# Softmax sums inverted by a power on GpSimd in fifteen slots, with a new table of the first 25 slots

## The chip, the core and the metric

The kernel runs on one core of a Trainium2 chip. The core has a tensor engine for matmuls (TensorE, PE in the profile, with its weight loads as PEld), VectorE (DVE), ScalarE (ACT), GpSimd (POOL), and queues for DMA transfers; here the SyncE queue (SP) issues nearly all of those. Each engine takes its own instructions strictly in the order in which they were issued to it, and waits where an input of the next one isn't there yet. The metric is the time of one execution on the device in microseconds, as the median of several runs. Lower is better.

## What is computed

The reference is an attention that keeps the 32 largest scores of each row, followed by a feed-forward block. Cut to what matters:

```python
# q, k, v: 8 batches, 8 heads, 576 rows, 64 wide
scores = np.matmul(q, k.transpose(0, 1, 3, 2)) / np.sqrt(64)
kth = np.partition(scores, -32, axis=-1)[..., -32:-31]
scores = np.where(scores >= kth, scores, -1e9)
attn = np.exp(scores - np.max(scores, axis=-1, keepdims=True))
attn = attn / (np.sum(attn, axis=-1, keepdims=True) + 1e-09)
x = np.matmul(attn, v)              # rearranged to 4608 rows of 512
h = x @ w_in                        # 512 x 2048
out = (h / (1 + np.exp(-1.702 * h))) @ w_out
```

The division by the sum (plus 1e-09) is the step that the change touches.

## The kernel before

**Slots.** The attention is cut into 144 slots of 128 query rows for two heads each, 18 per batch. For slot n, TensorE makes two heads' scores against all 576 keys (`scores`, line 468), in two PSUM banks of 288 keys each. ScalarE copies the second bank to SBUF, and the first too (`copy_scores`, 482; the tile `sc`, four buffers). VectorE pairs the two halves by maximum and minimum (`pair_up`, 489; tile `ranked`): this needs the scores of the first bank and ScalarE's copy of the second, and when it and the copies are done, the banks are free for the scores of a later slot. Then VectorE finds the 32 largest of each row in four rounds of MAX8 and MATCH_REPLACE8 (`topk`, 509; tile `top`). This search is most of VectorE's work.

**From the search to the values.** GpSimd works out the cut and the offset for the exponential (`bounds`, 534; tiles `cut` and `low`). ScalarE masks (`mask`, 549) and takes the exponentials (`exps`, 557; tile `pr`) and gives their sums (`den`). Then comes `invert` (568): GpSimd adds 1e-09 to the sums (tile `some`, 128x2), and VectorE takes the reciprocal (tile `rden`, 128x2). In slots 0 to 8 (`BY_DMA` is 8) `rden` goes into two diagonal matrices, and TensorE normalizes while it transposes the probabilities (`divide`, 575, and `turn`, 590). From slot 9 on GpSimd normalizes (`normalize`, 582, two passes over `pr`), ScalarE splits the result into 16-bit halves into the buffer of `sc` (`split`, 618), a DMA writes these to memory (`rows<-sc`), and a transposed read brings them back (`turn_by_dma`, 626, `pt<-rows`). The buffer of `sc` is free for the copy of a slot four later when that write has read it. TensorE multiplies with the values (`values`, 652, and its variants).

**The feed-forward block** runs beside it: blocks of 128 rows of x are multiplied with `w_in` in units (`hidden`, 789), ScalarE takes a tanh (`tanh`, 814), GpSimd or VectorE gate it (`gate`, 826) and form the sums of one step of Strassen's scheme (`combine`, 843), and TensorE multiplies with `w_out` or with sums of its quarters (`project`, 896). In the first slots the weights are loaded in pieces and rounded by ScalarE, GpSimd and VectorE (`round_piece`, 265), GpSimd then forms the sums of the quarters (`weight_sums`, 875), and TensorE fills its idle time with matmuls that nothing uses (`stay_warm`, 299).

**What sets the order.** The opening and slots 0 to 24 (`COLLECTED` is 25, line 33) are recorded: every call of an engine is put into a list of 2593 steps (lines 127 to 136), and `issue_in_order` (1678) then issues them in the order that the string `ORDER` (36) writes out, a table of step numbers and runs. An engine so gets its instructions in the order of the table. From slot 25 on the calls are issued as the program makes them, in pairs of slots (`joined_pair`, 1599). In the profile a recorded step has the line L133, every later one L132, so the two parts can be told apart.

In the recorded part, `invert(n)` is called in the middle of the search of slot n + 1 (`find`, 1303, or `slot`, 1174), and its two operations are two steps that the table places apart from each other.

Of the kernel before, what the change touches and what calls it, by code (L numbers as in the profile page):

```python
# [9 lines left out]
ALU = mybir.AluOpType  # L10
ENG = mybir.EngineType
F32 = mybir.dt.float32
# [7 lines left out]
P = 128  # L20
# [12 lines left out]
COLLECTED = 25  # L33
# [112 lines left out]
def kernel(  # L146
# [27 lines left out]
    nc = Engines(tc.nc)  # L174
# [25 lines left out]
    BY_DMA = 8  # L200
# [50 lines left out]


    pieces = [(c, g) for g in range(NG) for c in range(CC)] + [(None, f) for f in range(FC)]
    raw = {}

    def load_piece(n):
        c, g = pieces[n]
# [1480 lines left out]
```

## Time and profile before

| | |
|---|---|
| median of 3 runs | 1342.28 us (1342.17 to 1343.64) |
| profiled execution | 1342.64 us, its span 1340.9 us |
| mean granted clock of TensorE | 0.996 |
| PE, DVE, ACT, POOL busy | 1326.5, 1266.9, 1158.4, 978.6 us |
| last VectorE instruction of the table ends | 241.7 us |
| reciprocals on VectorE | 144: 24 at L133, 120 at L132 |

Busy time counts an engine from the start to the end of each instruction. Matmuls are pipelined and overlap, so a TensorE that is busy all the time can still have room; the number of passes in a stretch tells more. The span runs from the first to the last instruction; the execution has 1.7 us around it. A timeline row gives start, length, engine, line, operation, output and inputs, shapes and count, and in brackets the idle time of the engine just before it and what ended it. A row of waits gives who waited for whom, and then the total, the number of times and the longest.

### The profile page before, as it was taken

The page shows a single profiled execution, that of the slowest core. Times are in us where ns is not written, and L with a number is a line of the kernel's source. Part 1 is how long each engine was busy: PE and PEld are TensorE (multiplying, and loading weights), DVE is VectorE, ACT ScalarE, POOL GpSimd, SP SyncE. Part 2 cuts the span into 40 slices and gives each one's busy share as a digit, 9 for nine tenths or more (in the row PEclk, how much of TensorE's full clock was granted, in tenths as well). Part 3 has the DMA queues.
Part 4 walks back from the last instruction along what each step waited for, and adds up shares of the span by engine and source line. Part 5 has one row for each costly group of instructions (what it writes and reads, how often), then busy time and mean ns, then how long its engine had stood idle before and what let it go on. Part 6 is the DMA issues. An engine that isn't in the chain of part 4 may idle for free.

```text
span 1340.9 us, 54139 instructions
## 1 busy us (share of the span) xinstructions
PE 1326.5 (99%) x22528; PEld 1202.9 (90%) x22528; DVE 1266.9 (94%) x3371; ACT 1158.4 (86%) x1871; POOL 978.6 (73%) x1788
## 2 busy tenths in 40 slices
PE   8999999999999999999999999999999999999998
PEld 5777689899999999999999999999999999999998
DVE  7999999999999999999999999999999999999902
ACT  6999998999999988999999989899998988888831
POOL 3888987777777777777777777777777777777761
PEclk8999999999999999999999999999999999999999
DMA  7553878888998798989999787988999878755650
GB/s 239 173 169 119 191 182 201 213 191 205 218 219 195 169 206 195 236 191 202 205 220 205 184 188 181 235 199 195 186 228 214 199 158 170 189 140 145 149 116 18
DMA packets 532358, 249.27 MB, mean 186 GB/s; under 512 B 463760, under 2 KB 510352, under 8 KB 532112
## 3 DMA queue, kind: packets, MB, share of 16 engines
q1 hardware_dynamic: 531520, 245.38, 78.5%
q8 instruction: 176, 2.88, 0.9%
q14 instruction: 70, 0.57, 0.1%
q10 hardware_dynamic: 592, 0.43, 0.1%
HBM read 46.01 MB, written 104.60 MB: 112 GB/s over the span
## 4 chain that ended last, share of the span: by engine, by line
PE 94%; DVE 3%; DMA 1%; ACT 1%; SPq 1%; issue 0%; POOL 0%; DVEq 0%; ACTq 0%; POOLq 0%
PE unit L132 32%; PE po L132 29%; PE mixed L132 12%; PE s_ps L132 7%; PE po L133 6%; PE s_ps L133 2%; PE o L133 2%; PE tp L133 2%; PE ph L133 2%; DVE ranked L133 1%; DVE top L133 1%; DMA pt<-rows 1%; ACT sc L133 1%; DMA rows<-sc 0%; SPq L133 0%
## 5 line engine op out<-in xcount | busy, mean ns | idle before, releaser
L132 DVE MAX8 top<-ranked 128x8 f32<-128x288 f32 (+1 forms) x952 | 518.2, 596 | 0.0
L132 PE MATMUL unit<-xT,win 128*64 128x128 f32 x7936 | 454.3, 273 | 0.0
L132 PEld LDWEIGHTS unit<-xT,win 128*64 128x64 f32 x7936 | 437.4, 137 | 0.0
L132 DVE MATCH_REPLACE8 ranked<-top,ranked 128x288 f32<-128x288 f32 x714 | 384.1, 543 | 0.0
L132 PE MATMUL po<-wout,th 128*64 128x128 f32 x4032 | 330.0, 274 | 0.0
L132 POOL TENSOR_TENSOR th<-th,th 128x128 f32<-128x128 f32 x374 | 273.9, 732 | 29.9
L132 PE MATMUL po<-raws,th 128*64 128x128 f32 x3064 | 252.9, 273 | 0.0
L132 PEld LDWEIGHTS po<-wout,th 128*64 128x64 f32 x4032 | 238.3, 137 | 9.9 <-issue 5.1
L132 POOL TENSOR_SCALAR pr<-pr,rden 128x576 f32<-128x576 f32 x240 | 176.5, 745 | 75.2 <-DVE rden L132 75.2
L132 ACT COPY sc<-pr 128x2304 uint16<-128x2304 uint16 x96 | 205.5, 2140 | 1.2 <-POOL pr L132 1.2
L132 PEld LDWEIGHTS po<-raws,th 128*64 128x64 f32 x3064 | 184.6, 137 | 0.0
L132 ACT ACTIVATE th<-unit 128x512 f32<-128x512 f32 x124 | 74.9, 604 | 94.4 <-PE unit L132 94.4
L132 ACT ACTIVATE pr<-sc,low 128x576 f32<-128x576 f32 x192 | 148.1, 786 | 0.0
L132 ACT ACTIVATE sc<-sc,cut 128x576 f32<-128x576 f32 x192 | 140.7, 797 | 0.0
L132 PE MATMUL s_ps<-qk_t 64*64 64x512 f32 x936 | 139.1, 596 | 1.4 <-ACT sc L133 0.8
L132 POOL TENSOR_SCALAR some<-den 128x2 f32<-128x2 f32 x120 | 26.5, 220 | 155.7 <-ACT pr L132 155.4
L132 DVE TENSOR_TENSOR ranked<-s_ps,sc 128x576 f32<-128x576 f32 x188 | 132.8, 748 | 0.0
L132 ACT COPY sc<-s_ps 128x1024 f32<-128x1024 f32 x93 | 95.6, 1028 | 33.8 <-PE s_ps L132 33.7
L132 POOL TENSOR_TENSOR th<-th 128x128 f32<-128x128 f32 x250 | 114.8, 459 | 0.4
L133 DVE MAX8 top<-ranked 128x8 f32<-128x576 f32 (+1 forms) x200 | 111.6, 598 | 0.0
L132 POOL TENSOR_TENSOR raws<-raws 128x128 f32<-128x128 f32 (+1 forms) x160 | 89.7, 569 | 8.1 <-ACT raws L132 3.0
L132 POOL TENSOR_SCALAR th<-th 128x512 f32<-128x512 f32 x124 | 76.5, 617 | 13.1 <-ACT th L132 13.1
(145 smaller groups left out, 2196.6 us busy)
## 6 DMA issues: line engine op xcount, KB each, us to landing
rows<-sc SPq DMA_DIRECT2D x112, 576.0 KB, 3.7
rows<-spare SPq DMA_DIRECT2D x24, 576.0 KB, 3.6
qk_rows<-pr SPq DMA_DIRECT2D x23, 576.0 KB, 4.9
out_dram<-raws SPq DMA_DIRECT2D x66, 128.0 KB, 3.1
raws<-in_moe_w_in_dram SPq DMA_DIRECT2D x16, 512.0 KB, 4.9
raws<-in_moe_w_out_dram SPq DMA_DIRECT2D x16, 512.0 KB, 3.8
qk_l<-in_q_dram SPq DMA_DIRECT2D x28, 256.0 KB, 4.6
qk_l<-in_k_dram SPq DMA_DIRECT2D x28, 256.0 KB, 4.8
```

The costliest lines, as they stand in the source:

```text
L132: return do(*args, **kwargs)
L133: self.engines.collected.append(lambda: do(*args, **kwargs))
```

## The change

There are two edits. In `invert`, for slots 9 to 23, the reciprocal on VectorE becomes a power on GpSimd, with an exponent tile of minus ones that is filled once at the start. Slots 0 to 8, and 24 and later, keep the reciprocal. And the table is another one: its first 165 steps are the same, and from there the 2593 steps, which are the same steps by number, stand in another order, by up to 201 places, on average 18 places away.

```diff
     pieces = [(c, g) for g in range(NG) for c in range(CC)] + [(None, f) for f in range(FC)]
     raw = {}
+    minus_one = const.tile([P, 2], F32, name="minus_one")
+    nc.gpsimd.memset(minus_one[:], -1.0)
...
         some = small.tile([P, 2], F32, name="some", tag="sums")
         nc.gpsimd.tensor_scalar(some[:], st[n]["den"][:], 1e-9, None, op0=ALU.add)
         rden = st[n]["rden"] = small.tile([P, 2], F32, name="rden", tag="inverse")
-        nc.vector.reciprocal(rden[:], some[:])
+        if BY_DMA < n < COLLECTED - 1:
+            nc.gpsimd.tensor_tensor(out=rden[:], in0=some[:], in1=minus_one[:], op=ALU.pow)
+        else:
+            nc.vector.reciprocal(rden[:], some[:])
```

The first lines of the table that differ, cut:

```diff
-208+4 130 163 156 213+4 166 157 131 167 159 132 194 191 168
+208+4 130 163 156 213+4 167 157 172+3 131 166 158 132 175 191 168
...
```

The order of the DMAs on the SP queue is the same row by row. On the other engines the order differs throughout the recorded part. What the prediction says of the new order it takes from the two orders written out engine by engine; for example, three of the places that it speaks of:

| ahead of it, number of steps | before | after |
|---|---|---|
| matmuls ahead of the last score of slot 8's first bank | 321 | 306 |
| the same for slot 10 | 402 | 386 |
| the same for slot 11 | 443 | 439 |
| ScalarE steps ahead of the copy of slot 24's second bank | 326 | 331 |
| VectorE steps, the 15 left out, ahead of slot 24's pairing | 422 | 428 |

160 rows, old and new, of the table ORDER are left out of this document.

## The prediction

> **What bounds the kernel now.** First the page: the head, the busy times and the chain of work that ended last.
>
> ```profile
> span 1340.9 us, 54139 instructions
> PE 1326.5 (99%) x22528; PEld 1202.9 (90%) x22528; DVE 1266.9 (94%) x3371; ACT 1158.4 (86%) x1871; POOL 978.6 (73%) x1788
> PE 94%; DVE 3%; DMA 1%; ACT 1%; SPq 1%; issue 0%; POOL 0%; DVEq 0%; ACTq 0%; POOLq 0%
> ```
>
> The chain is nearly all TensorE. But the change lies in the part that the table orders, and that part must be read by itself. A helper's line tells the two apart: what the table issues stands at L133, everything later at L132. Three stretches, two in the table and one across its end:
>
> ```profile
> 20.00:110.00 90.00, 85.15 (x717) 62.20 (x715) 87.70 (x236) 84.97 (x167) 77.61 (x100) 0.96 0.55 175
> 110.00:180.00 70.00, 70.00 (x685) 50.27 (x679) 69.61 (x187) 68.47 (x120) 63.69 (x85) 1.00 0.71 182
> 180.00:246.00 66.00, 64.43 (x1172) 57.14 (x1168) 64.89 (x174) 60.15 (x95) 50.44 (x93) 1.00 0.78 189
> ```
>
> The columns are PE, PEld, DVE, ACT, POOL. In 110 to 180 us VectorE works 69.61 of 70 us and ScalarE 68.47. TensorE's full figure hides room: 685 matmul passes in 70 us against 1172 in the next 66. So in the table VectorE sets the pace, with ScalarE close behind. Then the chain of waits across the end of the table, in order of time (start, length, what):
>
> ```profile
> 219.73 2.01 ACT sc L133
> 221.76 4.57 DMA rows<-sc
> 226.43 0.65 ACT sc L133
> 227.10 1.19 DVE ranked L133 x2
> ...
> 244.37 1.85 DVE ranked L132 x4
> ...
> 246.27 1.09 PE s_ps L132 x8
> ```
>
> From 227.10 to 246.2 us the chain is VectorE, row after row; TensorE starts its scores at 246.27, right after VectorE has paired slot 26. From there on the chain is TensorE's, which has most of the 94% above. What VectorE gains up to 246 can therefore become gain of the whole kernel, one for one, as long as TensorE and ScalarE can also be there earlier. What VectorE waits for in the table:
>
> ```profile
> DVE ranked L133 <- PE s_ps L133: 1.5, 3, 1.0
> DVE ranked L133 <- ACT sc L133: 1.5, 2, 0.9
> DVE wout L133 <- ACT wout L133: 0.4, 1, 0.4
> DVE rden L133 <- POOL some L133: 0.2, 1, 0.2
> DVE win L133 <- POOL win L133: 0.2, 1, 0.2
> ```
>
> That is 3.8 us after the first 20 us, and all that a better order could take from VectorE.
>
> **The change, part by part.** Removed: 15 of the reciprocals that stand in VectorE's queue.
>
> ```profile
> L133 DVE RECIPROCAL rden<-some x16: 144/152/167, 111.5 to 236.8; 128x2 f32<-128x2 f32 x16
> ```
>
> ```profile
> 129.44 0.15 DVE L133 RECIPROCAL rden<-some 128x2 f32<-128x2 f32 x1
> 129.50 1.10 DVE L133 MAX8 top<-ranked 128x8 f32<-128x576 f32 x2
> ```
>
> One takes 0.152 us, but the next instruction starts 0.06 us after it (129.44 to 129.50): neighbours overlap. By such starts one costs 0.06 to 0.08 us of the queue; I take 0.07, so 15 x 0.07 = **1.05 us**. The bounds are 15 x 0.06 = 0.9 and 15 x 0.152 = 2.3 us.
>
> Moved: the table. I counted in the two built orders, engine by engine, what stands ahead of each score pairing, at VectorE's five largest waits that the new order touches:
>
> ```profile
> 81.27 0.76 DVE L133 TENSOR_TENSOR ranked<-s_ps,sc 128x576 f32<-128x576 f32 x1 [0.19 <-PE s_ps L133]
> 101.77 0.76 DVE L133 TENSOR_TENSOR ranked<-s_ps,sc 128x576 f32<-128x576 f32 x1 [0.95 <-PE s_ps L133]
> 110.39 0.76 DVE L133 TENSOR_TENSOR ranked<-s_ps,sc 128x576 f32<-128x576 f32 x1 [0.40 <-PE s_ps L133]
> 225.29 0.17 DVE L133 RECIPROCAL rden<-some 128x2 f32<-128x2 f32 x1 [0.25 <-POOL some L133]
> 227.10 0.76 DVE L133 TENSOR_TENSOR ranked<-s_ps,sc 128x576 f32<-128x576 f32 x1 [0.86 <-ACT sc L133]
> ```
>
> At 81.27, 101.77 and 110.39 (pairings of slots 8, 10 and 11) the scores that are waited for have 15, 16 and 4 fewer matmuls ahead of them on TensorE, and the pairings 2, 2 and 1 more instructions ahead on VectorE. Both sides open the gap, so these waits should go. The wait at 225.29 goes with its reciprocal. The wait at 227.10 (slot 24) came through ScalarE's copy at 226.43, which waited for the write of 4.57 us that started after a split; in the new order a second split (2.1 us) and four small ones stand between, so the write is covered, and VectorE has six more instructions ahead of the pairing. Sum: 0.19 + 0.95 + 0.40 + 0.25 + 0.86 = **2.65 us**.
>
> Not free: ahead of the pairings of slots 12 to 25 the new order puts about as much more on ScalarE as on VectorE. At slot 23 it is three instructions each, some 2 us; so when VectorE comes earlier by its reciprocals, ScalarE's copy is late unless ScalarE gains too, and in 110 to 180 it has only 1.5 us of idle time. New waits are bounded by 0 and by what is gained, 3.7 us. I take 1.3, a third of the 3.8 that VectorE waits for today, since most counted gaps there stay open by 0.6 us or more and that of slot 23 closes.
>
> Added: 15 powers of a 128x2 tile on GpSimd, an operation that no row shows, and one small fill at the start, where GpSimd's first small scaling comes at 20.0 us only (its row stands under the rivals). The order of the DMA queue on SP is the same to the row. The nearest row in size is the subtraction of two 128x2 tiles; the dearest of GpSimd's forms is the sign pass:
>
> ```profile
> L133 POOL TENSOR_TENSOR low<-cut 128x2 f32<-128x2 f32 x15 | 2.9, 193 | 0.3
> ...
> L133 POOL TENSOR_SCALAR raws<-raws 128x512 f16<-128x512 f32 x4 | 5.4, 1354 | 0.3
> ```
>
> So one costs between 0.19 and 1.35 us; I take 0.3, near the row of its size. Queued behind it are the two normalizing passes of the slot, then the split on ScalarE, its write and the transposed read. In slots 9 to 18 this path has no room to spare: the split starts 0.03 to 0.26 us after the second pass. The first and the last of the seven of these ten slots that are tight:
>
> ```profile
> 129.12 0.22 POOL L133 TENSOR_SCALAR some<-den 128x2 f32<-128x2 f32 x1
> 130.02 0.76 POOL L133 TENSOR_SCALAR pr<-pr,rden 128x576 f32<-128x576 f32 x1
> 130.95 0.75 POOL L133 TENSOR_SCALAR pr<-pr,rden 128x576 f32<-128x576 f32 x1
> 131.95 2.13 ACT L133 COPY sc<-pr 128x2304 uint16<-128x2304 uint16 x1
> ```
>
> ```profile
> 195.69 0.22 POOL L133 TENSOR_SCALAR some<-den 128x2 f32<-128x2 f32 x1 [0.94 <-ACT pr L133]
> 196.43 1.47 POOL L133 TENSOR_SCALAR pr<-pr,rden 128x576 f32<-128x576 f32 x2 [0.53 <-DVE rden L133]
> 198.04 2.11 ACT L133 COPY sc<-pr 128x2304 uint16<-128x2304 uint16 x1
> ```
>
> From the end of the sum to the first pass is 130.02 - 129.34 = 0.68 us, from the last pass to the split 131.95 - 131.70 = 0.25: a room of 0.93. At slot 18 it is 0.52 + 0.14 = 0.66. For slots 11, 13, 14, 16 and 17, worked the same way, it is 0.45, 0.37, 0.91, 0.87 and 0.60. At 0.3 us a power fits into every room and the detour over VectorE's queue is saved; nothing is late. GpSimd itself has 70 - 63.69 = 6.3 us of idle time in 110 to 180, against 8 x 0.3 = 2.4.
>
> **The sum**: -1.05 - 2.65 + 1.3 = -2.4 us. The profiled execution took 1342.64 us, 1.7 more than its span and 0.36 more than the median 1342.28: it becomes 1340.2, and the median **1339.9**. 0.2% is 2.7 us, about what a measurement of this kernel tells from no change; the line is at 1339.6.
>
> **Rivals.**
>
> The order leaves no new wait: -1.05 - 2.65 = -3.7, so 1338.6, and 1337.4 if the remaining 1.15 us of the 3.8 go too (3.8 + 1.05 = 4.85). For it: at every pairing but one the counted gap stays open. Against: ScalarE has to gain as much as VectorE.
>
> TensorE can't follow. Just past the table it stood still twice:
>
> ```profile
> PE s_ps L132 <- ACT sc L133: 0.8, 1, 0.8
> PE s_ps L132 <- DVE ranked L132: 0.6, 1, 0.6
> ```
>
> If its own work holds it before that, only these 1.4 us go: 1340.9. For it: 180 to 246 holds 1172 passes in 66 us, nearly twice the density of the stretch before. Against: it has room ahead of 180, if its inputs come.
>
> The change doesn't do what it says: the new order's own waits eat the 3.7 us, and the time stays at 1342.3. For it: the present order also leaves 3.8 us of waits.
>
> The power is long; this is the rival on the other side. Its place is between the sum and the first normalizing pass of slots 9 to 18. At 1.35 us it exceeds the seven rooms by 0.42 + 0.90 + 0.98 + 0.44 + 0.48 + 0.75 + 0.69 = 4.66 us, by which ScalarE's splits, and all that is queued behind them, come late; ScalarE has no idle time for that, its score copies come late, and the waits that the table took away return. 4.66 - 1.05 = +3.6, so 1345.9. It decides from 0.8 us on, where the excess (0.35 + 0.43 + 0.20 + 0.14 = 1.1) eats what the reciprocals gave. For it: nothing here shows what a power costs on GpSimd. Against: the two small forms there, sums and differences, take 0.2.
>
> The first power alone is dear. The first of GpSimd's small scalings took 0.41 us where the median is 0.23:
>
> ```profile
> L133 POOL TENSOR_SCALAR cut<-top x25: 217/226/414, 20.0 to 241.8; 128x4 f32<-128x4 f32 x25
> ```
>
> So a first use costs 0.2 us here, once, and slot 9 has 3.0 us of room, worked as above; only a first use of more than that would show, and one of 5.4 us would take the forecast's 2.4 away: 1342.3. The Trainium skill, GPSIMD Engine Reference, section Instruction dispatch, says that the first call to a freshly loaded GpSimd kernel pays some 6 us for its code with no instruction to be seen in the profile. By that rule slot 9 would be about 3 us late and the time an estimated 1342.9; the trace's first use, 0.2 us more, does not bear it out for operations that are resident, and whether the power is one no run here shows.
>
> **How the numbers follow.** Forecast 0.37, its own range 1338.6 to 1341.2; no new wait 0.20; TensorE can't follow 0.17; nothing comes of it 0.07; a dear first use 0.03; a long power 0.16. Faster by over 0.2%: 0.20 and four tenths of the forecast, 0.35. Slower: 0.16 and the edge of "nothing comes of it", 0.17. Within: 0.48. The range goes from 1337.6, near the end of the best rival, to 1345.9, the long power at its bound, since that cost is the one with ends far apart.
>
> **What would show it.** VectorE's reciprocals at L133: 9 in place of 24. The power's own row on GpSimd: 0.2 to 0.5 us, and "POOL pr <- DVE rden" at L133 gone. VectorE's waits at L133 after 20 us: 3.8 now, 2.5 expected in all (1.15 old, 1.3 new), those for slots 8, 10, 11 and 24 gone. The first scores after VectorE's pairing of slot 26 at 243.9 in place of 246.27. A row of 0.8 us or more for the power with ScalarE idle before its splits would make the forecast wrong; so would the pairing of slot 26 on time but TensorE's long run not earlier.

## The result, and the profile after

The changed kernel took **1345.92 us** (median of 14 runs, 1344.09 to 1347.35) beside 1342.61 us of the kernel before in the same session (14 runs, 1341.62 to 1346.10). The ratio is **1.0018, 95% interval 1.0011 to 1.0025**: slower by about 2.4 us (1.5 to 3.4; the two medians lie 3.3 apart), where 2.4 us faster was forecast. The profiled execution took 1345.05 us. Its page, in the lines that answer to those of before:

```profile
span 1343.2 us, 54145 instructions
PE 1328.6 (99%) x22528; PEld 1204.9 (90%) x22528; DVE 1266.8 (94%) x3356; ACT 1157.9 (86%) x1871; POOL 993.0 (74%) x1804
PE 95%; DMA 1%; ACT 1%; DVE 1%; POOL 0%; SPq 0%; issue 0%; DVEq 0%; ACTq 0%
```

VectorE has 15 instructions fewer and GpSimd 16 more, as the diff says, but VectorE's share of the chain fell from 3% to 1%. The same three stretches (columns PE, PEld, DVE, ACT, POOL):

```profile
20.00:110.00 90.00, 84.21 (x678) 62.19 (x677) 87.51 (x235) 82.30 (x161) 77.95 (x97) 0.95 0.54 175
110.00:180.00 70.00, 70.00 (x661) 49.43 (x658) 68.20 (x177) 67.23 (x118) 65.38 (x89) 1.00 0.71 172
180.00:246.00 66.00, 64.94 (x1196) 58.38 (x1193) 64.79 (x167) 60.52 (x99) 60.66 (x108) 1.00 0.81 196
```

VectorE works less in 110 to 180 us (68.20 where it was 69.61) without having got further: no time was won, only work. The inverse, on both engines:

```profile
L133 POOL TENSOR_TENSOR rden<-some,minus_one x15: 708/719/728, 119.5 to 239.3; 128x2 f32<-128x2 f32 x15
L133 DVE RECIPROCAL rden<-some x9: 139/152/167, 25.8 to 113.6; 128x2 f32<-128x2 f32 x9
```

One power takes 0.719 us, more than twice the 0.3 that I took, and its shortest and longest are 0.02 us apart. What VectorE waits for from 20 to 250 us (us in all, times, longest), and the waits of 0.3 us and more one by one (the bracket is the wait ahead of the instruction):

```profile
DVE ranked L133 <- ACT sc L133: 3.4, 4, 1.1
DVE ranked L133 <- ACT xT L133: 1.4, 1, 1.4
DVE rden L133 <- POOL some L133: 0.6, 2, 0.4
```

```profile
43.60 0.76 DVE L133 TENSOR_TENSOR ranked<-s_ps,sc 128x576 f32<-128x576 f32 x1 [1.09 <-ACT sc L133]
52.96 0.76 DVE L133 TENSOR_TENSOR ranked<-s_ps,sc 128x576 f32<-128x576 f32 x1 [0.77 <-ACT sc L133]
100.22 0.17 DVE L133 RECIPROCAL rden<-some 128x2 f32<-128x2 f32 x1 [0.36 <-POOL some L133]
112.91 0.76 DVE L133 TENSOR_TENSOR ranked<-s_ps,sc 128x576 f32<-128x576 f32 x1 [1.37 <-ACT xT L133]
124.21 1.42 DVE L133 TENSOR_TENSOR ranked<-s_ps,sc 128x576 f32<-128x576 f32 x2 [0.42 <-ACT sc L133]
232.79 0.76 DVE L133 TENSOR_TENSOR ranked<-s_ps,sc 128x576 f32<-128x576 f32 x1 [1.10 <-ACT sc L133]
```

In all 5.4 us, where it was 3.8. The row of slot 11 (112.91) names ScalarE's `xT`, but that copy ended at 112.51 and TensorE's scores only at 112.80, so it waited for the scores, as before. The waits of slots 8 and 10 (0.19 and 0.95) are gone. In their place stand slots 4 and 5 (1.09 and 0.77; slot 4 had 0.62), 11 (1.37, was 0.40) and 12. Four of these six lie ahead of the first power at 119.5 us, and the wait of slot 24 is still there. The chain across the end of the table:

```profile
213.85 2.00 ACT sc L133
215.87 3.38 DMA rows<-sc
219.27 8.82 DMA pt<-rows
...
228.23 2.46 PE o L133 x75
...
248.50 1.09 PE s_ps L132 x8
```

Before, this stretch of the chain was VectorE's, from the pairing of slot 24 to slot 26. Now it runs from the split of slot 19 through its write and a transposed read of 8.82 us to TensorE's products with v at 228.23, and then along TensorE without a pause. The scores that came at 246.27 us come at 248.50. From there nothing differs: the span grew by 2.3 us, the scores came 2.23 us later. The whole loss is made in the table.

For the runs below I measure the table so: from VectorE's first pairing to the first unit product behind the table.

```profile
9.26 1.42 DVE L133 TENSOR_TENSOR ranked<-s_ps,sc 128x576 f32<-128x576 f32 x2 [2.78 <-ACT sc L133]
250.61 3.66 PE L132 MATMUL unit<-xT,win 128*64 128x128 f32 x63
```

```profile
9.62 1.42 DVE L133 TENSOR_TENSOR ranked<-s_ps,sc 128x576 f32<-128x576 f32 x2 [2.78 <-ACT sc L133]
252.84 1.37 PE L132 MATMUL unit<-xT,win 128*64 128x128 f32 x22
```

That is 241.35 us before and 243.22 after, 1.9 longer. It is one profiled execution of each kernel; the start of the table varies by 1.5 us between executions and the wait of slot 4 with it, from none to 1.3 us, so differences under half a microsecond say nothing here. Part of these 1.9 is VectorE's lost time (starts further apart than is usual for their form, in steps of over 0.12 us): up to 130 us 5.1 in place of 3.2, behind that 1.2 in place of 1.3.

### The profile page after: what moved, and what is told of

The parts are those of the page before. It is cut to its first block, busy times and chain, and to the rows that moved or that the text cites. A ratio compares the mean times of both kernels' runs of the same rounds, so it can differ in the third digit from the quotient of the medians.

```text
span 1343.2 us, 54145 instructions
## 1 busy us (share of the span) xinstructions
PE 1328.6 (99%) x22528; PEld 1204.9 (90%) x22528; DVE 1266.8 (94%) x3356; ACT 1157.9 (86%) x1871; POOL 993.0 (74%) x1804
## 4 chain that ended last, share of the span: by engine, by line
PE 95%; DMA 1%; ACT 1%; DVE 1%; POOL 0%; SPq 0%; issue 0%; DVEq 0%; ACTq 0%
PE unit L132 32%; PE po L132 29%; PE mixed L132 12%; PE s_ps L132 7%; PE po L133 7%; PE s_ps L133 2%; PE o L133 2%; PE ph L133 2%; PE tp L133 2%; DMA pt<-rows 1%; ACT sc L133 0%; DVE ranked L133 0%; DVE top L133 0%; SPq L132 0%; DMA rows<-sc 0%
## 5 line engine op out<-in xcount | busy, mean ns | idle before, releaser
L133 DVE MAX8 top<-ranked 128x8 f32<-128x576 f32 (+1 forms) x200 | 111.4, 599 | 0.0
```

Source lines behind the costliest of these rows:

```text
L133: self.engines.collected.append(lambda: do(*args, **kwargs))
```

## The experiments

Each kernel was run beside the kernel before on the same chip. "Length" is the table's length less 241.35, from the profiled execution. The last column is VectorE's wait at the pairing of slot 24. pow_old_table and recip_new_then_old were executed 5 times, the others 10 or 11 times. A table that takes fewer lines moves the line numbers: the recorded steps then stand at L128.

| run | inverse, slots 9 to 23 | order up to 134 us / behind | ratio [95%] | length, us | slot 24, us |
|---|---|---|---|---|---|
| changed kernel | power | new / new | 1.0018 [1.0011, 1.0025] | +1.9 | 1.10 |
| pow_old_table | power | old / old | 1.0035 [1.0022, 1.0047] | +3.8 | 1.78 |
| recip_new_table | reciprocal | new / new | 1.0016 [1.0008, 1.0025] | +1.9 | 0.81 |
| mult_new_table | product | new / new | 1.0011 [1.0002, 1.0020] | +1.1 | 0.92 |
| mult_old_table | product | old / old | 1.0006 [0.9998, 1.0015] | 0.0 | 1.68 |
| recip_old_then_new | reciprocal | old / new | 1.0000 [0.9991, 1.0008] | +0.1 | 0.30 |
| recip_new_then_old | reciprocal | new / old | 1.0037 [1.0025, 1.0050] | +4.1 | 1.00 |
| pow_old_then_new | power | old / new | 1.0013 [1.0004, 1.0022] | +1.6 | 1.57 |
| mult_old_then_new | product | old / new | 1.0004 [0.9995, 1.0013] | +1.3 | 2.10 |
| after_v_first | power | new / new | 1.0027 [1.0017, 1.0036] | +3.2 | none |
| pow_old_then_new_v_first | power | old / new | 1.0019 [1.0010, 1.0028] | +2.2 | none |
| recip_old_then_new_v_first | reciprocal | old / new | 1.0019 [1.0009, 1.0028] | +4.6 | 0.51 |
| mult_old_then_new_v_first | product | old / new | 1.0006 [0.9997, 1.0015] | +0.8 | none |
| before_no_v | reciprocal | old / old | 0.9994 [0.9985, 1.0002] | -0.5 | none |
| after_no_v | power | new / new | 0.9997 [0.9988, 1.0006] | +0.6 | none |
| mult_old_no_v | product | old / old | 1.0000 [0.9991, 1.0009] | +0.2 | 0.63 |
| mult_old_then_new_no_v | product | old / new | 0.9992 [0.9984, 1.0001] | -1.0 | none |
| before_sp_order | reciprocal | old / old | 0.9991 [0.9982, 1.0000] | -1.4 | none |
| after_sp_order | power | new / new | 1.0013 [1.0004, 1.0022] | +1.5 | none |

In the four runs whose names end in v_first the wait stands one slot earlier: 2.67, 2.40, 3.44 and 1.78 us at slot 23, in the order of the table.

### The operation and the order apart

The power with the order of before, the reciprocal with the new order, and both orders with a short product, which leaves the inverse out:

```diff
-            nc.gpsimd.tensor_tensor(out=rden[:], in0=some[:], in1=minus_one[:], op=ALU.pow)
+            nc.gpsimd.tensor_tensor(out=rden[:], in0=some[:], in1=minus_one[:], op=ALU.mult)
```

> The power on GpSimd in slots 9 to 23, but the table of the kernel before. Theory P (the power's own 0.72 us, on the path from the sums to the split, is what costs): slower than before, by the excess of 0.72 us over the tight rooms less the 1.05 us of the reciprocals, and the split's lateness going on into the score copies: +1 to +3 us, 1343.5 to 1345.5. Theory T (the new order is what costs): the old order keeps its few waits, and VectorE loses 15 reciprocals: 1341.5 to 1342.8, the same as before or a little faster.

> The reciprocal on VectorE everywhere, as before, but the new table. Theory P: the order's own gain of 2.65 us less its new waits shows, 1340.5 to 1342. Theory T: the new order's waits (5.4 us on VectorE against 3.8) stay and the 1.05 us of the reciprocals come back on top: 1346 to 1347.5.

> The new table, with a product in place of the power: it is about 0.2 us long where the power has 0.72; the normalization of slots 9 to 23 is left out of the result in that way (their sums are multiplied by minus one). Theory P: what was forecast for a power of 0.2 to 0.3 us, 1339 to 1341. Theory T: about as the changed kernel, 1344.5 to 1346.

> The old table, with the same product in place of the power (the inverses of slots 9 to 23 are left out). It has the shortest path from the sums to the normalizing passes and none of the 15 reciprocals. Both theories: not slower than before, 1341 to 1342.5. The difference to the power with the old table is the price of the power's length in that order: under P 1 to 3 us, under T under 1 us.

Neither theory alone held. The new order with the reciprocal of before, on VectorE as ever, is already 1.0016: the order costs 2.1 us without any power. And the power in the old order costs 4.7 us, 3.9 more than a product there (1.0035 less 1.0006). In the new order the same step from the product to the power is 0.9 us, less than the intervals can tell from none. Where VectorE waits in the old order with the power, one by one from 130 us on:

```profile
130.89 0.76 DVE L133 TENSOR_TENSOR ranked<-s_ps,sc 128x576 f32<-128x576 f32 x1 [0.30 <-ACT sc L133]
136.19 1.29 DVE L133 TENSOR_SCALAR wout<-wout 128x512 uint32<-128x512 uint32 x2 [0.49 <-ACT wout L133]
168.87 0.76 DVE L133 TENSOR_TENSOR ranked<-s_ps,sc 128x576 f32<-128x576 f32 x1 [1.06 <-ACT sc L133]
...
201.89 1.42 DVE L133 TENSOR_TENSOR ranked<-s_ps,sc 128x576 f32<-128x576 f32 x2 [0.65 <-ACT sc L133]
231.05 0.76 DVE L133 TENSOR_TENSOR ranked<-s_ps,sc 128x576 f32<-128x576 f32 x1 [1.78 <-ACT sc L133]
```

Each is a wait for something of ScalarE's. ScalarE's own waits for GpSimd's normalizing passes, from 110 to 247 us, are first those with the power and then those with the product:

```profile
ACT sc L133 <- POOL pr L133: 5.3, 9, 1.1
```

```profile
ACT sc L133 <- POOL pr L133: 1.5, 4, 0.6
```

These are the splits of slots 9 to 18. The power makes them wait 3.8 us more in all, and what is queued behind a split on ScalarE is a copy of scores that VectorE then waits for. Of the wait at slot 24 only 0.1 us is the power's: with the product it is 1.68. The product run tells of the other term. GpSimd's form is short there and the 15 reciprocals are off VectorE, yet the length is that of before to 0.0 us:

```profile
L133 POOL TENSOR_TENSOR rden<-some,minus_one 128x2 f32<-128x2 f32 x15 | 2.9, 194 | 0.5
```

```profile
228.67 0.76 DVE L133 TENSOR_TENSOR ranked<-s_ps,sc 128x576 f32<-128x576 f32 x1 [1.68 <-ACT sc L133]
```

The wait at slot 24, 0.86 us before, is 1.68 here: VectorE arrives earlier and waits longer. By the times this run is not told from the kernel before (0.9998 to 1.0015).

### Which half of the new order loses

A mixed table takes the steps of one order up to step 1273 (the fourth removal of slot 13, at 134.9 us before) and then what is left in the other:

```diff
-    order = new
+    order = old[: old.index(1273) + 1]
+    order += [i for i in new if i not in order]
```

> The reciprocal in all slots; the table of before up to step 1273 (the fourth removal of slot 13, at 134.9 us in the trace of before), and from there the steps that are left in the order of the new table. Theory E (the new order loses its time before 130 us: VectorE's lost time there is 5.0 us against 3.3 with the old table, and behind it 0.95 against 1.3): 3.3 + 0.95 lost on VectorE, 0.35 less than before, and 9.28 us in place of 8.86 from VectorE's end to the joined section's first unit: 0.1 us above the kernel before, ratio 1.000. Theory L (the loss lies in the later slots or in the whole): about +2.0 us as with the whole new table, ratio 1.0015.

> The reciprocal in all slots; the new table up to step 1273 (134.3 us in the trace of the new table with the reciprocal), and from there the steps that are left in the order of the old table. Theory E: 5.0 + 1.3 us lost on VectorE against 4.5 before, and 8.86 us to the first unit: +1.8 us, ratio 1.0013. Theory L: no change, ratio 1.000.

> The power in slots 9 to 23; the old table up to step 1273, then the new one. Theory E: 3.3 + 1.3 us lost on VectorE and 1.0 us of reciprocals gone, then 0.4 more to the first unit: 0.5 us below the kernel before, ratio 0.9996. If the power needs the new order of slots 9 to 12 as well (with the old table VectorE lost 1.5 us at 131 to 136 us): +1.0 us, ratio 1.0007. Theory L: as the changed kernel, ratio 1.0018.

> A product by a constant in the power's place (so the inverses of slots 9 to 23 are left out); the old table up to step 1273, then the new one. Theory E: 3.3 + 1.1 us lost on VectorE, 1.0 us of reciprocals gone, 0.4 more to the first unit: 0.7 us below the kernel before, ratio 0.9995. If taking the reciprocals off VectorE gains nothing whatever the order: ratio 1.000 to 1.0006. Theory L: as the new table with the product, 1.0011.

With the early half of before, the reciprocal's loss is gone (1.0000): the new order's loss comes mostly from ahead of 134 us. The split of slot 19 shows it too. Counted from the first pairing it ends at 206.1 us with the whole new order (recip_new_table) and at 204.9 with the mixture, which is 1.3 of the 1.8 us between their lengths; the other 0.5 is the write and the transposed read behind it.

The traces show where that part of the new order is late first. In all seven runs with it, TensorE's transposes of slot 0 wait for the second of the slot's two diagonal matrices (`xT<-ident,rden` on GpSimd), ahead of which the new order has two more rounding steps of the weights. In the changed kernel this matrix also takes 1.31 us where the others take 0.37, while VectorE does three rounding steps (29.33 to 30.41 us):

```profile
30.70 3.78 PE L133 MATMUL tp<-xT,pr 128*128 128x128 f32 x16 [3.75 <-POOL xT L133]
```

These transposes start 20.3 to 21.1 us after the first pairing in those seven runs, and 18.5 to 18.8 in the thirteen with the old order in this half, where they don't wait for the matrix. In the changed kernel the chains that end with the scores of slots 4, 5 and 11 go back through this wait. No run moves these steps alone, so how much of the loss comes from them is not shown. (GpSimd makes 16 such matrices, two a slot, so for slots 0 to 7; slot 8 already goes by GpSimd's passes and the DMA.)

The reverse mixture lost even more than the new order, with a wait of 1.76 us for the sum of slot 12 that neither order has by itself, so it bounds nothing. With the power and with the product, however, the mixture gave less than expected. VectorE is early in both, and slot 24 takes it back, 1.57 and 2.10 us. In the run with the product, what SP's queue did ahead of that pairing:

```profile
214.26 0.35 SPq L128 DMA_DIRECT2D rows<-sc  x1
214.66 1.33 SPq L128 DMA_DIRECT2D v_l<-in_v_dram  x1
216.10 1.35 SPq L128 DMA_DIRECT2D v_e<-in_v_dram  x2
217.70 7.13 SPq L128 DMA_TRANSPOSE pt<-rows  x1
224.88 0.58 SPq L128 DMA_DIRECT2D rows<-sc  x1
```

The write of slot 19, the load of v for the second batch, the transposed read of slot 19 and the write of slot 20 stand in one queue. The read holds it 7.13 us and lands 9.80 us after its start, at 227.50. The split of slot 20 had ended at 219.38 + 2.14 = 221.52; its write, which frees a buffer of scores, is issued 3.4 us after that. It lands at 228.57. The products that wait for the read come late too, and on ScalarE the copy of their result stands ahead of the copy of the scores of slot 24. This wait ends last:

```profile
229.21 0.27 ACT L128 COPY xT<-o 128x128 f32<-128x128 f32 x1 [2.84 <-PE o L128]
```

The read sets more than slot 24. In the six runs so far with the new order behind 134 us, the changed kernel among them, the first unit behind the table starts 24.74 to 24.75 us after the landing of this read, which itself moves between 226.62 and 228.09 us.

### The load of v ahead of the write

```diff
 SP's steps, in the order of the table
-1897 2044 2045 2046 2047 2048
+1897 2045 2046 2047 2044 2048
```

(1897 is a transposed read of q and k, 2044 the write and 2048 the transposed read of slot 19, 2045 to 2047 the loads of v.)

> The changed kernel; in its table only the three loads of v for the second batch (steps 2045 to 2047) stand ahead of the write of slot 19 (step 2044) on SP instead of behind it. Theory D (in the new order the end of the table hangs on the transposed read of slot 19, which took 8.82 us beside the load of v; TensorE stood still 1.06 us for it, and from there to the first unit it is 24.61 us without a pause in every run with the new late order): v is there before the read starts, the read takes 5 to 6 us, the 1.06 us go, and the time is 1.0 us below the changed kernel, ratio 1.0011. Theory V (VectorE and ScalarE hold the end in any case): no change, ratio 1.0018.

> The power, the old table to step 1273 and then the new one, with the three loads of v ahead of the write of slot 19. Theory D: TensorE's 1.49 us for the read of 9.08 us go: 1.5 us less than without this edit, ratio 1.0002. Theory V: ratio 1.0013 as without it.

> The reciprocal, the old table to step 1273 and then the new one, with the three loads of v ahead of the write of slot 19. Theory D: TensorE's 0.65 us for the read of 7.29 us go: ratio 0.9995. Theory V: 1.000 as without it.

> The product by a constant in the power's place (the inverses of slots 9 to 23 are left out), the old table to step 1273 and then the new one, with the three loads of v ahead of the write of slot 19. Theory D: TensorE's 1.56 us for the read of 9.80 us go, and what VectorE saves by 15 reciprocals fewer is no longer waited away at slot 24 (2.10 us there): 1.5 us less than without this edit, ratio 0.9993, below the same order with the reciprocal. Theory V: 1.0004 as without it.

All four missed; none got faster. SP's queue in the changed kernel with this edit:

```profile
212.01 2.66 SPq L128 DMA_TRANSPOSE qk_t<-qk_rows  x1
214.71 0.59 SPq L128 DMA_DIRECT2D v_l<-in_v_dram  x1
215.35 2.50 SPq L128 DMA_DIRECT2D v_e<-in_v_dram  x2
217.90 0.71 SPq L128 DMA_DIRECT2D rows<-sc  x1
223.86 2.89 SPq L128 DMA_TRANSPOSE pt<-rows  x1
```

The transposed read now takes 2.89 us of the queue, as meant. But the loads start only behind the read of q and k and hold the queue to 217.85, so the write of slot 19, whose split was done at about 216.0, is issued at 217.90, and then takes 223.86 - 217.90 = 6.0 us beside the load in place of 3.4. VectorE waited 2.67 us for the scores of slot 23. The collision was moved, not removed. In three of the four runs the read of slot 19 lands no more than 0.2 us earlier, counted from the first pairing, so they don't test theory D; with the product it lands 1.3 us earlier and the table is 0.5 us shorter. What speaks for theory D is the 24.74 to 24.75 us of the section before. (The profiled execution with the reciprocal was its slowest run, 1348.70; its length is not typical.)

### The load left out

```diff
         for i in order:
-            steps[i]()
+            if i not in (2045, 2046, 2047):
+                steps[i]()
```

> The kernel before without the three loads of v for the second batch in the table (steps 2045 to 2047 aren't issued; slots 18 and up then multiply with v of the first batch). Theory S (a transposed read that runs beside the load of v, 4.8 to 7.1 us on SP's queue where others hold it 2.5 us, makes the next slot's write late, and with it the copy of the scores of slot 24): the write of 4.57 us and the read get shorter, VectorE's 0.86 us at slot 24 go, ratio 0.9994. Theory V (VectorE and ScalarE set the end, SP doesn't): 1.000.

> The changed kernel without the same three loads of v. Theory S: TensorE's 1.06 us and VectorE's 1.10 us of waiting behind the read of 8.82 us go, 1.1 us less than the changed kernel: ratio 1.0010. Theory V: 1.0018 to 1.0022 as the changed kernel.

> The product by a constant in the power's place (inverses of slots 9 to 23 left out), the table of before, without the three loads of v. Theory S: VectorE's 1.68 us at slot 24 go, and the 1.05 us of the reciprocals that they hid show: 1.0 us below the kernel before without v, ratio 0.9987. If VectorE's saving is lost elsewhere: as the kernel before without v, 0.9994. Theory V: 1.0006 as with the loads.

> The product by a constant, the old table to step 1273 and then the new one, without the three loads of v. Theory S: TensorE's 1.56 us and VectorE's 2.10 us of waiting go: 1.6 us less than with the loads, ratio 0.9992. Theory V: 1.0004 as with them.

Three of the four got faster, the way of theory S. The changed kernel gained more than S has it (1.0010). Its interval and that of the mixture leave out theory V; that of the kernel before (0.9985 to 1.0002) does not. The mixture with the product, without the load:

```profile
214.50 0.36 SPq L128 DMA_DIRECT2D rows<-sc  x1
217.92 2.83 SPq L128 DMA_TRANSPOSE pt<-rows  x1
221.78 0.34 SPq L128 DMA_DIRECT2D rows<-sc  x1
```

The read holds the queue 2.83 us in place of 7.13, the write of slot 20 goes out 0.03 us after its split, slot 24 waits for nothing, and the length is 1.0 below that of before. That is as much as the 15 reciprocals, but the load's own part is in it: the kernel before gains 0.5 without the load, and the mixture with reciprocals and without the load was not run. In the kernel before, the write of slot 20 was not late, as theory S has it (the split ends at 221.73 us, the write starts at 221.76), but long: it took 4.57 us, and without the load 2.78. The changed kernel without the load is at 0.9997; the load had cost it 0.0021, some 2.8 us by the times and 1.3 by the lengths. The third run missed: with the old order the product gains nothing even now (1.0000 where before without the load is 0.9994). Its profile shows a wait of 0.63 us at slot 24 and smaller ones at slots 21 and 25, all for ScalarE's copies. So in the old order VectorE waits away at ScalarE's copies what the reciprocals gave.

### The load kept, its place changed

```diff
 SP's steps, in the order of the table
-1897 2044 2045 2046 2047 2048 2219
+2045 2046 2047 2044 2048 2219 1897
```

(2219 is the write of slot 20. The loads stand right behind the last product with the old v.)

> The kernel before with four of SP's steps moved in its table: the three loads of v for the second batch directly behind the last product with the old v (step 2005), ahead of the write of slot 19, and the transposed read of q and k of the third batch (step 1897) from ahead of them to behind the write of slot 20. Nothing is left out. Theory S: the load of v starts some 4 us earlier and is through when the transposed read of slot 19 begins; that read holds SP's queue 2.5 us in place of 4.8, the write of slot 20 and the copy of the scores of slot 24 come on time: ratio 0.9994, as without the load. If the write of slot 19 is late again (as with the loads ahead of it and the read of q and k still before them): 1.000 or above.

> The changed kernel with the same four of SP's steps moved; nothing is left out. Theory S: TensorE's 1.06 us and VectorE's 1.10 us of waiting behind the read of 8.82 us go; ratio 0.9997 to 1.0002, as without the load, what remains against the kernel before in the same SP order (0.0003 to 0.0008) being the loss of the new order before 130 us less what the reciprocals give. If the write of slot 19 is late again: 1.0018 or above.

The kernel before in this SP order is the best of all runs: 0.9991, with an interval that just reaches 1 (0.9982 to 1.0000), so at most 0.2% and perhaps nothing; against the changed kernel it is clearly ahead. Its queue:

```profile
206.95 1.24 SPq L128 DMA_DIRECT2D v_l<-in_v_dram  x1
208.25 1.54 SPq L128 DMA_DIRECT2D v_e<-in_v_dram  x2
213.37 0.36 SPq L128 DMA_DIRECT2D rows<-sc  x1
217.60 2.54 SPq L128 DMA_TRANSPOSE pt<-rows  x1
221.97 0.36 SPq L128 DMA_DIRECT2D rows<-sc  x1
```

The load starts at 206.95, is clear of the read, and all of slot 24's wait goes. The loads and the read of q and k moved together, so the part of each is not told apart. In the changed kernel the edit missed: it gained 0.4 us of length, and 1.0013 is not told from 1.0018. There the products with the old v end later, the load starts at 212.08, and it collides with the write of slot 19, which went out at 216.51 and was through when the read began at 222.02, 5.5 us later. Without the load the changed kernel had 0.9997, so the load's place matters, but this order of products leaves no good place for it.

## Why the prediction was wrong, point by point

**The moved table, -2.65 us: the step that failed.** I took the five largest waits that the order touches and counted what stands ahead of each. Two went as counted (0.19 and 0.95), one went with its reciprocal (0.25), the other two grew: slot 11 from 0.40 to 1.37, slot 24 from 0.86 to 1.10. And waits came up where the kernel before had little and I had not counted: slots 4, 5 and 12 and two inverses. In place of -2.65 + 1.3 = -1.35 VectorE's waits grew by 5.4 - 3.8 = 1.6. The new order with the reciprocal alone is 2.1 us slower (1.0016) and the mixed table puts most of that ahead of 134 us. A count of instructions ahead has no times in it: at slot 11 the scores had four matmuls fewer ahead of them and yet came later. Why TensorE and ScalarE are later in slots 4 to 12 of the new order was not tried by a run and stays open; the traces point at slot 0, where TensorE waits up to 3.8 us for a matrix of GpSimd's. That place stood in none of my counts, which began from VectorE's waits.

**Slot 24 within that step.** I wrote that a second split covers the write. The order of SP's queue is the same to the row, as said, but I did not ask how long its rows take. The transposed read of slot 19 beside the load of v lands 8.82 us after its start in the changed kernel, without the load 6.25. ScalarE stands still 1.83 us, up to 229.80, for the products that wait for it, and the copies of scores come behind them; the write has landed at 229.28. So the read and its products, not the write, set slot 24 in the new order. No rival named it.

**The reciprocals, -1.05 us.** Their size was right: from each reciprocal's start to the start of the next instruction, the 24 in the table of before take 1.63 us and the 9 that are left take 0.63. But nothing of it reaches the end while ScalarE's copies hold slot 24: with the order of before the table's length is the same to 0.0 us. I had bounded this by "new waits", a third of 3.8; these runs say all of it. Only with the early half of before and without the load is the table 1.0 us shorter.

**The power, 0.3 us.** Mis-sized, at 0.719 within the bounds of 0.19 and 1.35. By the sum alone that would have changed nothing: the rival of the long power put the deciding point at 0.8. With the order of before it costs 3.9 us over a product at 0.72 already, so the point was wrong too. The rooms were taken one at a time from the present times, and by them a power of 0.72 us is late by 0.8 in all; the splits waited 3.8 us more than with the product, and those of slots 9 and 12, which I had counted as roomy, are among them (0.98 and 0.56 us). The new order bears most of that: the splits wait 0.5 us for GpSimd in the changed kernel, and the power costs 0.9 us over a product by the times, with intervals that overlap. So the mechanism of that rival was right for the old order; the changed kernel is slow mainly for other reasons. That its time falls on this rival's 1345.9, worked out for a power of 1.35 us, is luck.

**The dear first use.** The first power:

```profile
119.50 0.73 POOL L133 TENSOR_TENSOR rden<-some,minus_one 128x2 f32<-128x2 f32 x1
120.19 1.29 POOL L133 TENSOR_TENSOR th<-th,th 128x512 f32<-128x512 f32 x1
```

It takes what the others take. GpSimd worked up to 119.53 ahead of it, and the next instruction starts 0.69 us behind its start. The Trainium skill (GPSIMD Engine Reference, section Instruction dispatch) has some 6 us of code loading at the first call of a freshly loaded kernel; this trace shows none for the power.

**TensorE can't follow.** Half seen. From 228.23 us to the first unit TensorE has no pause in the new order, so there its own work does hold the end. But what makes it late is the wait for the transposed read ahead of that, which the rival did not name.

**The sum by the lengths**: -1.0 for the reciprocals, +1.9 lost ahead of 130 us, -0.1 behind it, +0.4 from VectorE's end to the first unit (9.3 us where it was 8.9) = +1.2, against the measured +1.9. The other 0.7 lies in steps of VectorE too small to place.

**What was to show it.** Reciprocals at L133: 9, as said, and GpSimd's waits for the inverse there (3.8 us before) are gone. The power's row is outside 0.2 to 0.5. The waits are 5.4, not 2.5. The scores behind slot 26 came at 248.50, not 243.9.

## What to carry to other kernels

Taking work off the busiest engine gains only what the next wait lets through: look for the wait that the engine would reach earlier, and ask what sets its end, down to the DMA queue. A new order is judged at all its waits and in times, not at the old order's waits and by ranks. Where one queue issues loads, writes and transposed reads in turn, ask of each how long it holds the queue beside the others and when it lands, and keep large loads clear of a write that frees a buffer.

## What the runs showed of the hardware

- A power of a 128x2 f32 tile on GpSimd takes 0.719 us, a product of the same shape 0.194.
- The transposed read of slot 19 (`pt<-rows`) held SP's queue 4.8 to 7.1 us and landed 7.3 to 9.8 us after its start where the load of v (1024 KB and two of 128 KB) was issued just ahead of it, and 2.5 to 2.9 and 6.1 to 6.9 where that load was left out. The read of slot 18, issued behind two writes of q and k, held it 2.3 to 4.2 us without any load of v beside it. Issued behind the load of v, the write of slot 19's split took 5.5 to 6.1 us in five runs and 4.2 in the one where the load was nearly through, against 3.4 in the changed kernel.
- A reciprocal of 0.152 us took 0.07 us of VectorE's time, from its start to the next start (24 of them 1.63 us).
